# Part of an attention's exponentials on VectorE, a scan in two halves, and zero matmuls sized per group

## The chip, the cores and the metric

One core of a Trainium2 chip. The metric is the device time of one execution in microseconds (us); the median of three runs of the kernel before is 1030.11 us (1026.20 to 1030.48). TensorE does the matrix products and writes to PSUM, ScalarE the exponentials, VectorE most of the elementwise work; SyncE's queue (SP) issues nearly all transfers.

## What is computed

The output mixes two branches of one input `x` (2048 positions, 512 channels) by a gate per position:

```python
g = sigmoid((x * gate_w).sum(-1, keepdims=True))
# a: attention, 32 heads of 16 channels
q, k, v = split(x @ wqkv)
a = (softmax(q @ k.T * 16 ** -0.5) @ v) @ wo
# b: a state-space convolution, 128 complex states for each channel
K[d, l] = sum_n (C * dB)[d, n] * exp(dt * A)[d, n] ** l     # real part
b = causal_conv(x, K) + x * Dskip
return g * a + (1 - g) * b
```

## The kernel before

**Attention.** The 32 heads are worked in 32 blocks of 4 heads by 512 queries. A block has 16 key tiles of 128 keys, and each key tile has four score tiles (one for each head) of 128 keys x 512 queries: 2048 *slots* in all. Three slots make a *group*, 683 groups. `qk` (L662) computes the three score tiles of a group into one of two PSUM banks of 1536 columns, SC0 and SC1, with matmuls that use 32 rows of the array each and run side by side. `ex` (L673, instruction L675) lets ScalarE take the exponential of the whole bank into ET, a ring of 15 tiles (NS). `pv` (L678) multiplies the four tiles of a key tile with the values, 32 columns of the array each, and adds them up in the bank OA over the block; a column of ones among the values gives the sum of the exponentials. At the block's end `norm_a` to `norm_c` (L688 to L697) transpose OA on VectorE, divide, and store to OnT. There is one OA, so the next block's first `pv` waits for `norm_a`.

**State-space branch.** VectorE makes parameters and powers (`params` L756, `base` L854, `table` L892). `kstage` (L946) and `sstage` (L969) form kernels and chunk states with small matmuls into the one shared bank MB, VectorE moves them out (L958, L986, L988), and they go through DRAM. `sload` (L1004) brings the states of a block of 32 channels back, transposed, into SG0 or SG1, which hold a quarter of the channels each. `scan` (L1023) runs 31 steps for each of four quarters on VectorE: G = G * MU + state, complex, in four tensor-tensor instructions of 128x256 fp32 and one cast back to SG (L1040 to L1053). `ystage` (L1090) multiplies the scanned states (SG) and the inputs (X2, loaded by `ublocks` L1139) with the tables, `yread` brings the result back, `combine` and `outs` (L1173, L1195) mix it with the attention's output projection.

**The order of the work** is a list schedule made on the host (`Prog`, `Sched`, L37 to L355). Every instruction has a modelled cost `c` and latency; the program of each engine is then fixed. The main loop (L1325) places, for each group, the exponential, the next score set, and then lets `fill` (L325) pick steps of the other generators that can start by the time ScalarE is modelled to end, by their priority (0 and 1: attention and projections; 2 to 6: the rest). After that it may place zero matmuls (L1342): 128x128 zeros times 512 zero columns, added to OA. They change no value. How many is decided by `lack`: FILL (1400) columns for each group less the weighted columns `a` of the group's own matmuls (512 for a full array, 128 for a score or value matmul), and only while a block's OA is open. All matmuls are issued by L551.

`place` (L462) lays the buffers into SBUF by the groups in which they live; buffers that share bytes add waits.

Of the kernel before, what the change touches and what calls it, by code (L numbers as in the profile page):

```python
# [8 lines left out]
INT32 = mybir.dt.int32  # L9
AF = mybir.ActivationFunctionType  # L10
# [13 lines left out]
FILL = 1400  # L24
NS = 15
SGH = 144
# [3 lines left out]
class Buf:  # L30
# [18 lines left out]
    def int(self, off, dims):  # L49
        return self(off, dims).bitcast(INT32)  # L50

# [4 lines left out]
class Prog:  # L56
# [61 lines left out]
    def ready(self, a):  # L118
        eng, R, W = a[1][0], a[1][2], a[1][3]
        t = 0.0  # L120
        for acc, wr in ((R, False), (W, True)):
            for b, sl, *tag in acc:
# [5 lines left out]
                for d in (st[0], st[1]) if wr else (st[0],):  # L128
                    for s, i in d.items():
                        if s != "PE" or eng != "PE":  # L130
                            t = max(t, self.fin[(s, i)] + (0 if s == eng else .08))
# [29 lines left out]
    def op(self, eng, fn, R=(), W=(), c=.1, lat=.05, a=0):  # L161
# [8 lines left out]
        for s, k in deps.items():  # L170
            at = max(at, self.fin[(s, k)] + (0 if s == eng else .08))
# [63 lines left out]
class Sched:  # L235


    def __init__(self, prog):
        self.p = prog
        self.thr = []  # L240
        self.flag = set()
        self.lock = {}
        self.now = None
        self.n = 0

# [79 lines left out]
    def fill(self, until, pe_until):  # L325
        while True:
            best = None
            for t in self.thr:
# [3 lines left out]
                if t.eng == "PE":  # L332
                    if e + t.cost > pe_until and t.up > 0 or e > pe_until:
                        continue
# [31 lines left out]
def declare(nc, es):  # L366
# [11 lines left out]
    sb("ET", NS * 512)  # L378
    for k in range(4):
        sb(f"OnT{k}", S)  # L380
# [57 lines left out]
    sb("G", 2 * 128, FP32)  # L438
    for n in ("s2", "s3"):
        sb(n, 2 * 128, FP32)  # L440

    sb("X2", 4 * 32 * 64)
# [19 lines left out]
def place(nc, bufs):  # L462
# [20 lines left out]
    for k in range(400):  # L483
# [7 lines left out]
        if best is None or top < best[0]:  # L491
            best = (top, order)
    assert best[0] <= end, (best[0] - end, live(sbs))
# [38 lines left out]
def dv(n, r=1):  # L532
    return .1 + n * 1.045e-3 / r


def record(nc, p, B, ins):
# [10 lines left out]
    MM, QUAD, TRI = .23, .34, .33  # L547
# [85 lines left out]
    def proj_ev(kind, idx, c, bank):  # L633
# [3 lines left out]
           [(o, ky)], c=.65)  # L637

    def vproj_mm(pi, kq, i, q4):
        kt = 4 * kq + i  # L640
        mm(lambda: MB(128 * i, [[1, 128]]), lambda: xT(q4 * S + 128 * kt, [[1, 128]]), lambda: B["Wv"](q4 * D + 128 * pi, [[1, 128]]),
           [xk(kq, q4), (B["Wv"], 0)], [(MB, 0, ('p', "V", pi, kq))], q4 == 0, q4 == 3, c=.08, a=128)

    def vproj_ev(pi, kq):
        op("DVE", lambda v: v.tensor_copy(VE((pi * 16 + 4 * kq) * VW, [[VW, 4], [17, 8], [1, 16]]),
                                          MB(0, [[128, 4], [16, 8], [1, 16]])),
           [(MB, 0, ('p', "V", pi, kq))], [(VE, (pi, 4 * kq + i)) for i in range(4)], c=.68)

    def mk_qm(b):
        qc, pi, w = b // 8, (b % 8) // 2, b % 2  # L650
        op("DVE", lambda v: v.tensor_scalar(Qm(512 * (b % 2), [[1, 512]]), B[f"Q{qc}"](512 * pi, [[1, 512]]),  # L651
                                            msk(w, [[1, 1]]), None, ALU.mult), [(B[f"Q{qc}"], pi), (msk, 0)], [(Qm, b % 2, b)], c=.32)
# [19 lines left out]

    def ex(g):  # L673
        sc, e, n = SC[g % 2], (3 * g) % NS, len(slots(g))
        op("ACT", lambda a: a.activation(ET(512 * e, [[1, 512 * n]]), sc(0, [[1, 512 * n]]), AF.Exp, scale=DH ** -0.5),  # L675
           [(sc, i, g) for i in range(n)], [(ET, s % NS, s) for s in slots(g)], c=.063 + .4267 * n, lat=.1)

    def pv(q):  # L678
        b, kt = divmod(q, 16)
        pi, w = (b % 8) // 2, b % 2  # L680
        for j in range(4):
            hh, e = 2 * j + w, (4 * q + j) % NS
            mm(lambda j=j: OA(0, [[1, 512]], 32 * j, 32), lambda hh=hh: VE((pi * 16 + kt) * VW + 17 * hh, [[1, 32]]),
               lambda e=e: ET(512 * e, [[1, 512]]),
               [(VE, (pi, kt))] + [(ET, (4 * q + i) % NS, 4 * q + i) for i in (range(4) if j == 0 else [j])],
               [(OA, 0, b)], kt == 0, kt == 15, pos=(0, 32 * j), c=QUAD if j == 0 else 0, a=128)

    def norm_a(b):  # L688
        op("DVE", lambda v: v.transpose(OT(0, [[1, 512]]), OA(0, [[1, 512]])), [(OA, 0, b)], [(OT, 0, b)], c=.72)  # L689

    def norm_b(b):
# [3 lines left out]
                                            Rz(16 * w, [[1, 16], [0, 16]]), ALU.mult), [(OT, 0, b), (Rz, w)], [(ON, w)], c=.4)  # L695

    def norm_c(b):  # L697
        qc, pi = b // 8, (b % 8) // 2
        op("DVE", lambda v: v.transpose(OnT[qc](pi * 512, [[1, 512]]), ON(0, [[1, 512]])), [(ON, 0), (ON, 1)],
           [(OnT[qc], pi)], c=.7)  # L700
# [153 lines left out]
    def base(qr, eng):  # L854
# [4 lines left out]
        for l, n in ((0, "VV"), (1, "VL")):  # L859
            yield (eng, .38)  # L860
            op(eng, lambda v, l=l, n=n: v.tensor_copy(FP(l, [[e8, 2], [8, 128]]), B[n](d0, [[D, 2], [1, 128]])), key(n), [(FP, 0)], c=.38)
# [30 lines left out]
    def table():  # L892
# [3 lines left out]
        for pb in range(NBLK // 2):  # L896
# [9 lines left out]
            for i in range(2):  # L906
                yield ("DVE", .4)
                op("DVE", lambda v, i=i, b0=b0, B16=B16: v.tensor_copy(PT(i * PTN, [[CB * T, 2], [T, CB], [1, 16]]),
                                                                     B16(b0 + i * CB * 16, [[2048, 2], [16, CB], [1, 16]])), bk, [W[i]], c=.38)
# [21 lines left out]
    X2 = B["X2"]  # L931
# [37 lines left out]
    def sstage(blk):  # L969
        yield ("AFTER", f"ub{blk // 4}")  # L970
        q0, qr, bl = (blk % 2) * PTN, blk // 4, blk % 4
        for bank in range(4):
# [3 lines left out]
            for pp in range(2):  # L976
                yield ("PE", .29)
                for j in range(4):
                    k, par = 4 * bank + 2 * pp + j // 2, j % 2
                    mm(lambda pp=pp, j=j: MB(256 * pp, [[1, 256]], 32 * j, 32),  # L980
                       lambda k=k, par=par: X2(2048 * qr + 16 * bl + k, [[64, 32]], 64 * par, 64),
                       lambda k=k, par=par: Qt(q0 + 128 * k, [[16 * 128, 2], [1, 128]], 64 * par, 64),
                       [(Qt, (blk % 2, k // 8), blk), (Qt, (blk % 2, 2 + k // 8), blk), (X2, (qr, par))], [(MB, 0, ('S', blk, bank))], pos=(64 * par, 32 * j),
                       c=.29 if j == 0 else 0, a=32)
            yield ("DVE", .8, -1)
            op("DVE", lambda v, bank=bank: v.tensor_copy(Sst(512 * bank, [[256, 2], [1, 128]]), MB(0, [[256, 2], [1, 128]])),  # L986
               [(MB, 0, ('S', blk, bank))], [(Sst, bank, (blk, bank))], c=.37)
            op("DVE", lambda v, bank=bank: v.tensor_scalar(Sst(512 * bank + 128, [[256, 2], [1, 128]]), MB(128, [[256, 2], [1, 128]]),  # L988
                                                           -1.0, None, ALU.mult),
               [(MB, 0, ('S', blk, bank))], [(Sst, (bank, 1), (blk, bank))], c=.37)  # L990
# [13 lines left out]
    def sload(blk):  # L1004
# [3 lines left out]
        if qr < 2:  # L1008
            yield ("AFTER", "K15" if qr else "K3")
        else:  # L1010
            yield ("AFTER", f"yq{qr - 2}")
        sg = SG[qr % 2]
        if bl == 0:
# [3 lines left out]
        dma("SP", lambda e: e.dma_start_transpose(sg(2 * SGH + CB * bl, [[SGH, 64], [1, CB]]),  # L1017
                                                  sd.dram(CB * blk * 8192, [[8192, CB], [1, 8192]])),
            [(sd, (blk, i)) for i in range(4)], [(sg, bl, (qr, 'S'))], c=2.5, lat=3)
# [3 lines left out]
    def scan():  # L1023
# [4 lines left out]
        def quarter(qr):  # L1028
            sg, d0 = SG[qr % 2], 128 * qr
            ks = [(sg, bl, (qr, 'S')) for bl in range(4)]  # L1030
            for bl in range(4):
                yield ("AFTER", f"sg{4 * qr + bl}")
# [367 lines left out]
```

## Time and profile before

| | before |
|---|---|
| median of three runs | 1030.11 us |
| span of the profiled execution (first to last instruction) | 1023.2 us |
| median less span | 6.9 us |
| ScalarE busy | 946.5 us (93%) |
| TensorE busy | 866.9 us (85%) |
| VectorE busy | 611.4 us (60%) |
| mean granted TensorE clock | 0.690 |

The time of the profiled execution itself is not recorded beside its span; the median of the runs is taken as what stands around it. In the profile's rows `PE` is TensorE's matmuls, `PEld` its weight loads, `DVE` VectorE, `ACT` ScalarE, `SP` the queue of most transfers. A stretch's row has its bounds, its length, then for each engine the busy us and (x number of instructions), then the granted clock, the share of the DMA engines and GB/s. A row of a group has line, engine, operation, output <- inputs, shapes and count, then the busy us and the mean ns of one, then the idle time before it and what ended that.

### The profile page before, as it was taken

What the parts mean: (1) busy time and instruction counts of PE and PEld (TensorE: products, weight loads), DVE (VectorE), ACT (ScalarE), POOL (GpSimd) and SP (SyncE); (2) the same over time, 40 slices, a digit from 0 to 9 for tenths busy, and PEclk for the clock granted to TensorE, in tenths of its full rate; (3) what the DMA queues carried; (4) which work ended last, traced back from release to release, by engine and by line L of the source; (5) the groups of instructions that cost most, each with busy time, mean ns of one, the idle gap of its engine ahead of it and who ended that gap; (6) DMA issues with size and microseconds to landing.
All of it is one profiled execution on the core that took longest, in us unless ns stands there. A gap on an engine that the chain in (4) does not pass through costs nothing.

```text
span 1023.2 us, 17025 instructions
## 1 busy us (share of the span) xinstructions
PE 866.9 (85%) x7076; PEld 246.4 (24%) x7076; DVE 611.4 (60%) x1382; ACT 946.5 (93%) x693; POOL 11.9 (1%) x15
## 2 busy tenths in 40 slices
PE   7888788789889888889989899899887787787786
PEld 3332322112112222223323233233211111111111
DVE  4899999987678998878889988702310000000201
ACT  6999999999889999989999999999999899989985
POOL 4000000000000000000000000000000000000000
PEclk9999995555556887655565665755957766767757
DMA  8200005259997788696475725142100000000000
GB/s 180 83 2 1 2 1 83 103 119 202 232 240 176 170 186 208 187 176 165 108 145 145 168 75 148 40 124 48 42 11 11 1 1 1 1 1 1 1 1 21
DMA packets 228940, 92.21 MB, mean 90 GB/s; under 512 B 193408, under 2 KB 216576, under 8 KB 226816
## 3 DMA queue, kind: packets, MB, share of 16 engines
q1 hardware_dynamic: 227136, 90.22, 38.5%
q10 hardware_dynamic: 1728, 0.92, 0.4%
q8 instruction: 55, 0.90, 0.3%
q14 instruction: 21, 0.17, 0.0%
HBM read 27.92 MB, written 35.65 MB: 62 GB/s over the span
## 4 chain that ended last, share of the span: by engine, by line
ACT 51%; PE 41%; DVE 2%; SPq 2%; DMA 2%; issue 2%; ACTq 0%; DVEq 0%
ACT ET L675 51%; PE OA L551 19%; PE SC L551 14%; PE MB L551 9%; SPq L1017 1%; DMA Wq<-in_A_wqkv_dram 1%; DMA Qt<-gm_ptd 0%; SPq L937 0%; DVE Sst L986 0%; DMA Tt<-gm_kpd 0%; DVE Sst L988 0%; DVE OT L689 0%; DVE Kst L958 0%; SPq L994 0%; ACTq L555 0%
## 5 line engine op out<-in xcount | busy, mean ns | idle before, releaser
L675 ACT ACTIVATE ET<-SC 128x1536 bf16<-128x1536 f32 (+1 forms) x683 | 939.4, 1508 | 62.1 <-PE SC L551 55.7
L551 PE MATMUL OA<-ET,VE 128*32 128x512 bf16 x2048 | 268.6, 514 | 117.4 <-ACT ET L675 114.1
L551 PE MATMUL SC<-Qm,KT 32*128 32x512 bf16 x2048 | 353.2, 511 | 11.3 <-ACT ET L675 9.7
L551 PEld LDWEIGHTS SC<-Qm,KT 32*128 32x128 bf16 x2048 | 69.5, 95 | 275.9 <-issue 203.6
L551 PE MATMUL OA<-wm 128*128 128x512 bf16 x276 | 123.5, 573 | 1.2 <-DVE wm L604 1.2
L551 PEld LDWEIGHTS OA<-ET,VE 128*32 128x32 bf16 x2048 | 56.8, 100 | 268.9 <-ACT ET L675 242.0
L651 DVE TENSOR_SCALAR Qm<-Q,msk 128x512 bf16<-128x512 bf16 x31 | 10.6, 342 | 178.7 <-PE SC L551 178.7
L689 DVE STREAM_TRANSPOSE OT<-OA 128x512 f32<-128x512 f32 x32 | 22.9, 714 | 74.2 <-PE OA L551 74.1
L703 DVE TENSOR_TENSOR tt<-B,D 128x1024 bf16<-128x1024 bf16 x96 | 63.2, 683 | 0.3
L1050 DVE TENSOR_TENSOR G<-s,s 128x256 f32<-128x256 f32 x120 | 50.7, 422 | 3.4
L551 PE MATMUL MB<-Qt,X 64*32 64x256 bf16 x512 | 43.3, 392 | 8.8 <-issue 3.2
L1040 DVE TENSOR_TENSOR s<-G,MU 128x256 f32<-128x256 f32 x120 | 50.1, 417 | 0.1
L1046 DVE TENSOR_TENSOR s<-s,SG 128x256 f32<-128x256 f32 x120 | 50.1, 417 | 0.0
L1043 DVE TENSOR_TENSOR s<-G,MU 128x256 f32<-128x256 f32 x120 | 50.0, 417 | 0.0
L551 PE MATMUL MB<-Py,SG 128*32 128x64 bf16 x1024 | 44.1, 259 | 0.0
L1118 DVE CAST Yst<-MB 128x256 bf16<-128x256 f32 x32 | 13.5, 423 | 50.7 <-PE MB L551 50.5
L986 DVE CAST Sst<-MB 128x256 bf16<-128x256 f32 x64 | 27.0, 422 | 24.3 <-PE MB L551 23.8
L551 PEld LDWEIGHTS OA<-wm 128*128 128x128 bf16 x276 | 27.5, 119 | 57.4 <-issue 52.3
L1053 DVE CAST SG<-G 128x256 bf16<-128x256 f32 x120 | 34.9, 291 | 3.0
L551 PE MATMUL MB<-Tt,X 64*32 64x64 bf16 x512 | 35.7, 267 | 0.2 <-DMA Tt<-gm_kpd 0.2
L551 PEld LDWEIGHTS MB<-Py,SG 128*32 128x32 bf16 x1024 | 27.5, 150 | 34.9 <-issue 31.8
L703 DVE TENSOR_TENSOR ft<-FP,L 128x1024 f32<-128x1024 f32 (+1 forms) x32 | 33.8, 1079 | 0.0
(123 smaller groups left out, 470.2 us busy)
## 6 DMA issues: line engine op xcount, KB each, us to landing
gm_ptd<-PT SPq DMA_DIRECT2D x16, 1024.0 KB, 5.1
Py<-gm_ptd SPq DMA_DIRECT2D x32, 512.0 KB, 4.3
gm_sd<-Sst SPq DMA_DIRECT2D x64, 128.0 KB, 2.7
gm_kpd<-Kst SPq DMA_DIRECT2D x16, 256.0 KB, 4.3
Tt<-gm_kpd SPq DMA_DIRECT2D x128, 32.0 KB, 3.5
gm_xrd<-in_A_x_dram SPq DMA_DIRECT2D x1, 2048.0 KB, 12.1
X<-gm_xrd SPq DMA_DIRECT2D x8, 256.0 KB, 4.9
gm_ytd<-Yst SPq DMA_DIRECT2D x32, 64.0 KB, 4.0
```

The source lines that it names most:

```text
L551: op("PE", lambda t: t.matmul(out(), lhsT(), rhs(), start=start, stop=stop, skip_group_check=True, **kw), R, W, c=c, lat=.15, a=a)
L651: op("DVE", lambda v: v.tensor_scalar(Qm(512 * (b % 2), [[1, 512]]), B[f"Q{qc}"](512 * pi, [[1, 512]]), msk(w, [[1, 1]]), None, ALU.mult), ...
L675: op("ACT", lambda a: a.activation(ET(512 * e, [[1, 512 * n]]), sc(0, [[1, 512 * n]]), AF.Exp, scale=DH ** -0.5), [(sc, i, g) for i in ran ...
L689: op("DVE", lambda v: v.transpose(OT(0, [[1, 512]]), OA(0, [[1, 512]])), [(OA, 0, b)], [(OT, 0, b)], c=.72)
L703: op(eng, lambda v: v.tensor_tensor(o(), a(), b_(), f), R, W, c=c)
L986: op("DVE", lambda v, bank=bank: v.tensor_copy(Sst(512 * bank, [[256, 2], [1, 128]]), MB(0, [[256, 2], [1, 128]])), [(MB, 0, ('S', blk, ba ...
L1040: op(e, lambda v: v.tensor_tensor(s2(0, [[128, 2], [1, 128]]), G(0, [[128, 2], [1, 128]]), MU(d0, [[0, 2], [1, 128]]), ALU.mult), key("G", ...
L1043: op(e, lambda v: v.tensor_tensor(s3(0, [[128, 2], [1, 128]]), G(128, [[-128, 2], [1, 128]]), MU(D + d0, [[D, 2], [1, 128]]), ALU.mult), k ...
L1046: op(e, lambda v, so=so: v.tensor_tensor(s2(0, [[128, 2], [1, 128]]), s2(0, [[128, 2], [1, 128]]), sg(so, [[SGH, 2], [1, 128]]), ALU.add), ...
L1050: op(e, lambda v: v.tensor_tensor(G(0, [[1, 256]]), s2(0, [[1, 256]]), s3(0, [[1, 256]]), ALU.add), [(s2, 0), (s3, 0)], [(G, 0)], c=.38)
L1053: op(e, lambda v, so=so: v.tensor_copy(sg(so, [[SGH, 2], [1, 128]]), G(0, [[128, 2], [1, 128]])), key("G"), ks if c < NCH - 2 else [(sg, b ...
L1118: op("DVE", lambda v: v.tensor_copy(Yst(r2 * 256, [[1, 256]]), MB(0, [[1, 256]])), ky, [(Yst, r2, u)], c=.37)
```

## The change

- **Offload.** From group 440 (DV0) on, in two groups of three, and only in key tiles 1 to 13 of a block, the group's third tile is left out of the exponential: 130 tiles, gathered in 34 batches of up to four. For such a tile VectorE writes `XS * score + XB` as 16-bit integers into DZ (`bits`); read as bf16 these bits are 2^e (1 + f). For each batch it then makes m = (1 + f) / 2 with a mask, the product of both, and 2^e (1 + 1/128) with a second mask. The two bf16 terms, product and power, are multiplied with the values one after the other, into the same OA; their sum stands for the exponential. The last value set of a block waits for the block's batches.
- **Scan.** Two halves of 256 channels in place of four quarters of 128: half as many instructions, each twice as wide; SG holds a half. State loads wait for K7 or S15 in place of K3, K15 or the y-stage; X2 is four buffers, loaded one quarter at a time behind the S-stage.
- **Zero matmuls.** The wanted columns follow the modelled time of the group (1600 for 1.335 us); the debt is kept between -256 and 768; MB serves where no OA is open; zeros of 512 or 256 columns; `fill` keeps room for them. In 4 of 14 groups TensorE steps of priority 2 and 5 are held back and at least 1792 columns are wanted.
- Modelled costs and latencies in the schedule are other numbers; the output stage starts at group 480 in place of 400.

The core of the diff:

```diff
-FILL = 1400
+ZCOL = .213 / 512
+FILL = 1600
+OVER = .3
+REST = (14, 4, 1792)
-SGH = 144
+SGH = 272
+NB = 3
+XS = 128 * DH ** -.5 / math.log(2)
+XB = 128 * (127 - math.log2(2 * .7535040986732945))
+DV0 = 440
+DVP = (1, 1, 0)
+DVK = 14
...
+    for g in range(DV0, NG):
+        x = 3 * g + 2
+        if x < NSL and DVP[g % len(DVP)] and 0 < x // 4 % 16 < DVK:
...
     def ex(g):
         sc, e, n = SC[g % 2], (3 * g) % NS, len(slots(g))
+        if 3 * g + 2 in vec:
+            n = 2
...
+    def bits(g):
+        i, k = vec[3 * g + 2]
+        sc, r = SC[g % 2], i % NB
+        op("DVE", lambda v: v.tensor_scalar(DZ.u16(2048 * r + 512 * k, [[1, 512]]), sc(1024, [[1, 512]]), XS, XB, ALU.mult, ALU.add),
+           [(sc, 2, g)], [(DZ, (r, k), (i, k))], c=.61)
...
+    def batch(i):
+        n = 512 * len(order[i]["s"])
+        yield ("DVE", .07 + n / 3840)
+        mask(i, DU, 0x007F, 0x3F00, [(DU, i % NB, ("m", i))])
+        yield ("DVE", dv(n, 2))
+        square(i)
+        yield ("DVE", .07 + n / 3840)
+        mask(i, DZ, 0x7F80, 0x0001, [(DZ, (i % NB, k), (i, k, "t")) for k in range(len(order[i]["s"]))])
+        b = order[i]["b"]
+        yield ("AFTER", f"pv{16 * b}")
...
+        for t in (DU, DZ):
+            yield ("PE", QUAD)
+            for k, s in enumerate(order[i]["s"]):
+                key = (DU, i % NB, i) if t is DU else (DZ, (i % NB, k), (i, k, "t"))
+                pv_mm(s, t, 2048 * (i % NB) + 512 * k, [key], QUAD if k == 0 else 0)
...
-            sg, d0 = SG[qr % 2], 128 * qr
+            sg, d0 = SG[h], 256 * h
...
+            if kt == 15:
+                yield ("AFTER", f"dv{b}")
...
         t = p.tm["ACT"]
-        sch.fill(t, t + .35)
-        lack = min(lack, 1536) + FILL - p.act
-        b = sch.now
-        while lack > 256 and b is not None and p.tm["PE"] < t + .2:
-            mm(lambda: OA(0, [[1, 512]]), lambda: wm(0, [[1, 128]]), lambda: wm(0, [[1, 512]]), [(wm, 0)], [(OA, 0, b)], False, False)
-            lack -= 512
+        want = FILL * (t - t0) / 1.335 + min(max(lack, -256), 768)
+        t0 = t
+        sch.rest = g % REST[0] < REST[1]
+        if sch.rest:
+            want = max(want, REST[2])
+        sch.fill(t, t + OVER, want)
+        lack = want - p.act
+        p.act = 0
+        while lack >= 256 and p.tm["PE"] < t + OVER:
+            b = sch.now
+            if b is not None:
+                bank, W = OA, [(OA, 0, b)]
+            elif sch.lock.get("MB") is None:
+                bank, W = MB, [(MB, 0, "zero")]
+            else:
+                break
+            n = 512 if lack >= 512 else 256
+            mm(lambda bank=bank, n=n: bank(0, [[1, n]]), lambda: wm(0, [[1, 128]]), lambda n=n: wm(0, [[1, n]]), [(wm, 0)], W,
+               bank is MB, bank is MB, c=n * ZCOL, a=n)
+            lack -= n
```

More of the change, by code (lines that the diff above doesn't have):

```diff
@@ L929, in table @@
                 sch.add(kstage(blk), .5)
-    X2 = B["X2"]
+    X2 = [B[f"X2{k}"] for k in range(4)]
     def qload(blk):
@@ L1049, in quarter @@
[L1049 to L1056 removed]
+                yield (e, F5)
```

221 lines of the change are left out of this document (137 added, 84 removed).

## The prediction

> **What bounds the kernel now.** I read the page first: the span, the engines, the clock row, the chain.
>
> ```profile
> span 1023.2 us, 17025 instructions
> PE 866.9 (85%) x7076; PEld 246.4 (24%) x7076; DVE 611.4 (60%) x1382; ACT 946.5 (93%) x693; POOL 11.9 (1%) x15
> PEclk9999995555556887655565665755957766767757
> ACT 51%; PE 41%; DVE 2%; SPq 2%; DMA 2%; issue 2%; ACTq 0%; DVEq 0%
> ```
>
> ScalarE is busy for 93% of the span, yet the chain that ends last gives TensorE 41%: the two alternate, and TensorE's clock is full only at first. Next, the stretches view of the exponential's tile (ET), four stages between changes of clock; behind it the same stages for OA, the bank of the value matmuls and of the zero matmuls.
>
> ```profile
> core 0: us, PE busy (x) PEld busy (x) ACT busy (x), PEclk, DMA share, GB/s
> 14.50:154.90 140.40, 30.83 (x308) 7.93 (x308) 139.47 (x104) 1.00 0.11 27
> 154.90:298.30 143.40, 45.14 (x292) 8.31 (x292) 134.81 (x99) 0.51 0.72 163
> 298.30:650.60 352.30, 99.30 (x716) 20.54 (x716) 331.44 (x239) 0.63 0.70 157
> 650.60:1012.60 362.00, 92.46 (x728) 19.88 (x728) 332.74 (x244) 0.69 0.07 17
> ```
>
> ```profile
> 14.50:154.90 140.40, 30.83 (x308) 7.93 (x308) 3.00 (x5) 1.00 0.11 27
> 154.90:298.30 143.40, 46.17 (x294) 8.44 (x294) 3.56 (x5) 0.51 0.72 163
> 298.30:650.60 352.30, 143.09 (x814) 29.74 (x814) 7.83 (x11) 0.63 0.70 157
> 650.60:1012.60 362.00, 166.12 (x892) 36.66 (x892) 7.89 (x11) 0.69 0.07 17
> ```
>
> Time over exponentials gives each stage's pace: 1.350, 1.448, 1.474, 1.484 us per group of three tiles. At the full clock ScalarE runs end to end at 1.35; the later stages lose 143.4 - 99 x 1.35 = 9.8, 352.3 - 239 x 1.35 = 29.6 and 362.0 - 244 x 1.35 = 32.6 us: **72 us of excess**. The second fence minus the first counts the zero matmuls: 0, 2, 98, 164. So the projections held the clock in stage one, and when they ended nothing replaced them: the fill at L1339 keeps an unlimited debt, and the surplus of the projections postpones zeros for some 150 us.
>
> What one group costs at either clock is in the timeline of TensorE in the last stage, and the chain view says who waits.
>
> ```profile
> 870.22 0.61 PE L551 MATMUL SC<-Qm,KT 32*128 32x512 bf16 x3
> 870.76 1.89 PE L551 MATMUL OA<-wm 128*128 128x512 bf16 x4
> 872.58 0.61 PE L551 MATMUL SC<-Qm,KT 32*128 32x512 bf16 x3
> 873.12 0.41 PE L551 MATMUL OA<-ET,VE 128*32 128x512 bf16 x4
> 873.47 0.39 PE L551 MATMUL SC<-Qm,KT 32*128 32x512 bf16 x3
> ```
>
> ```profile
> ACT ET L675 <- PE SC L551: 55.7, 93, 3.4
> ```
>
> Start to start at half clock: a score set .54 (872.58 to 873.12), a zero 1.82 / 4 = .455; at full clock a set of four value matmuls .35. A burst of four zeros at half clock stands for 1.82 us ahead of the next scores, longer than one exponential: that is the wait of ScalarE, 55.7 us in 93 waits.
>
> **What moves the clock.** Stretches on the grid of the clock changes (3.41 us), all engines, then OA, then ET:
>
> ```profile
> 866.37:869.79 3.42, 1.91 (x22) 0.59 (x21) 0.00 (x0) 2.94 (x3) 0.00 (x0) 1.00 0.00 0
> 869.79:873.20 3.41, 3.41 (x18) 0.73 (x18) 0.00 (x0) 2.54 (x2) 0.00 (x0) 0.50 0.00 0
> 880.03:883.44 3.41, 2.24 (x20) 0.71 (x18) 0.35 (x1) 3.41 (x4) 0.00 (x0) 1.00 0.00 0
> ```
>
> ```profile
> 866.37:869.79 3.42, 1.01 (x13) 0.30 (x12) 0.00 (x0) 1.00 0.00 0
> 869.79:873.20 3.41, 2.46 (x12) 0.52 (x12) 0.00 (x0) 0.50 0.00 0
> 880.03:883.44 3.41, 1.46 (x11) 0.52 (x12) 0.00 (x0) 1.00 0.00 0
> ```
>
> ```profile
> 866.37:869.79 3.42, 0.89 (x12) 0.30 (x12) 2.94 (x3) 1.00 0.00 0
> 869.79:873.20 3.41, 0.58 (x8) 0.09 (x8) 2.54 (x2) 0.50 0.00 0
> 880.03:883.44 3.41, 0.80 (x8) 0.21 (x8) 3.41 (x4) 1.00 0.00 0
> ```
>
> I weigh each matmul by its share of the array: 128 columns for a score or value matmul, 512 for a zero, edges cut off. The first window (tail of one zero) carries about 2,400, and the next runs at half. The second (four zeros) carries about 3,200, and the next is full. The third (three zeros) about 3,400, and the clock stays. So the window's weighted work decides, with an edge between 2,400 and 3,200; I take 2,900 (an estimate), both to hold and to regain the full clock. Own work of 768 a group (six matmuls) gives 768 x 3.41 / 1.35 = 1,940: never enough alone.
>
> **The change part by part.** *Offload.* 130 groups drop their third tile from ScalarE. The lines view by source shows a two-tile exponential (the shortest) beside the usual three:
>
> ```profile
> L675 ACT ACTIVATE ET<-SC x683: 1023/1451/1863, 14.5 to 1012.6; 128x1536 bf16<-128x1536 f32 x171
> ```
>
> 1.451 - 1.023 = .428 us each, x 130 = **-55.6 us**, all in the last stage, provided nothing else sets the pace there.
>
> *New VectorE work.* Rows by shape:
>
> ```profile
> L636 DVE CAST KT<-MB 128x512 bf16<-128x512 f32 x15 | 10.3, 690 | 3.7 <-PE MB L551 3.3
> L741 DVE TENSOR_SCALAR u<-u 128x512 int32<-128x512 int32 x2 | 0.8, 416 | 0.0
> L908 DVE COPY PT<-B 128x1024 bf16<-128x1024 bf16 x16 | 6.3, 419 | 0.8 <-DMA gm_ptd<-PT 0.8
> L703 DVE TENSOR_TENSOR tt<-B,D 128x1024 bf16<-128x1024 bf16 x96 | 63.2, 683 | 0.3
> L1050 DVE TENSOR_TENSOR G<-s,s 128x256 f32<-128x256 f32 x120 | 50.7, 422 | 3.4
> L1053 DVE CAST SG<-G 128x256 bf16<-128x256 f32 x120 | 34.9, 291 | 3.0
> L703 DVE TENSOR_TENSOR u<-u,u 128x512 f32<-128x512 f32 x13 | 8.9, 685 | 0.2
> 650.00:1013.00 363.00, 299.47 (x2065) 76.53 (x2062) 50.64 (x114) 333.74 (x244) 0.00 (x0) 0.69 0.07 17
> ```
>
> The bits instruction reads 512 columns of PSUM: .69 as L636, x 130 = 90 us. The selection makes 34 batches (28 of four tiles, 6 of three). A mask over 2,048 16-bit elements has no row: twice L908 is .84, four times the bitwise L741 is 1.66, four times L636 is 2.76; below it can't be under L908's .42. I take .75, nearest to L908 (same element size, one source); a square is at most 2 x .683, I take 1.25. 34 x (2 x .75 + 1.25) = 94 us. Together 184 us on an engine that is busy for 50.6 of the last 363: 235 of some 290, so it fits, at a cost of 0, hidden by ScalarE's 1.02 to 1.45 per group. If that cover is gone it costs at once: the scores two groups on write the bank that the bits instruction reads, so they now wait for VectorE too, and behind a bits instruction that waits for its scores stand, in order, the batches, the norms and the evictions of MB, for which TensorE waits. The Trainium skill (VectorE: DVE Perf Modes, The perf-mode tier table) gives .693 us for a 2,048-element bf16 tensor_scalar in SBUF; by it the masks cost 47 instead of 51 us and the sum stays. No row here has 16-bit integers.
>
> *Scan on halves.* 120 steps of 4 x .42 + .29 = 1.97 become 60 steps of 4 x .685 plus a cast of .29 to .58 (I take .42): 236 to 190 us, 46 us of VectorE freed. ScalarE's wait list names TensorE alone, so this is worth 0 on the path; it makes room. The 16 state loads wait for more blocks (K7, S15), the 8 loads of X2 go from one burst to behind the S stage of earlier quarters; all stay on SP's queue, none is added, and what they pass there are table and Sst transfers with idle engines beside them after 700 us; the first scan starts later. I take 0, at most +5. The output stage moves from group 400 to 480, with 203 groups left for its 16 tiles: 0.
>
> *Added value matmuls.* 68 extra sets (two terms, 34 batches), 42 of which hit one array position twice: 26 x .35 + 42 x .55 = 32 us at full clock (.55 for two passes, an estimate between .35 and .70), twice that at half. A batch must end before its block's last value set, which waits for it; behind that stand all later scores, in order.
>
> *Sized zeros.* 1,600 columns for each 1.335 modelled us, debt cut to -256..768, MB as second bank, and 4 groups in 14 cleared of prio-2 and prio-5 TensorE steps and raised to 1,792. At full clock a window then carries 1,600 x 3.41 / 1.335 = 4,090, far over 2,900; the time is .35 + .26 + 1.6 x .23 = .98 of 1.35. At half: .54 + .41 + 1.6 x .455 = 1.69 us a group, 3,230 a window: over the edge, so one slow window should cure itself. In the last stage at full clock TensorE needs 243 x .61 = 148, 32 for the terms, and about 230 zeros x .23 = 53: 233 of 271 us.
>
> What is left of the excess: in the first 39.4 us I keep 17, for the waits inside TensorE's order, which the clock doesn't cure:
>
> ```profile
> PE MB L551 <- DVE Sst L988: 5.2, 9, 2.2
> PE MB L551 <- issue: 3.2, 3, 2.5
> PE MB L551 <- DVE Kst L959: 3.0, 6, 0.6
> ```
>
> (11.4 us, and 5.6 for the windows that they cool.) In the last 32.6 us I keep 18: about 1 us at each of 11 block ends, and 7 for two-tile groups, whose 1.02 us leave the next scores less room. So -22 and -15.
>
> **Sum**: 1023.2 - 55.6 - 22 - 15 = 931 us of span. The median of 1030.1 lies 6.9 above this span; 938.
>
> **The rivals.** *A, no excess at all*: 72 + 55.6 go, 1023.2 - 127.6 + 6.9 = 902. For it: stage one does it for 140 us. Against: block ends and late banks. By the Trainium skill (TensorE: Matmul & The Clock Gate, Part 1) one busy window opens the gate and it takes an idle one to close it; then A would hold. The row at 866.37 disagrees: 1.91 us busy of 3.42, in pieces, and the next window is at .50.
>
> *B, the last stage's clock stays at .69*, because batches and block ends keep breaking the windows. At half clock TensorE needs 231 + 62 + 105 = 398 us there, 1.64 a group; mixed by time (.62 half, at 1.64; .38 full, at 1.16) 243 groups take 344 us, 18 less than now: 1023.2 - 22 - 18 + 6.9 = 990.
>
> *C, slower: the zeros are fixed in the program and are paid at half clock.* With S- and y-stage matmuls a half-clock group of the third stage costs about 1.9 us (1.69, and .2 for these, an estimate). Weighted by time the clock is .635 over the last three stages, so half clock holds (1 - .635) / .5 = .73 of it. With that share kept, stage two takes 99 / (.73 / 1.69 + .27 / 1.36) = 157 us, 14 more; stage three 239 / (.73 / 1.9 + .27 / 1.36) = 410, 58 more; the last 344, 18 less: 1023.2 + 54 + 6.9 = **1084**. It decides at a half-clock share of about .5, where the same three quotients add up to the 858 us of now. Against it: 3,230 to 4,090 a window. For it: third-stage groups at half clock carry only 1,600 x 3.41 / 1.9 = 2,870, about the edge.
>
> *D, masks at one element per cycle* (2.76): VectorE needs 235 + 137 = 372 us in the last stage and sets its pace: 938 + 82 = 1020.
>
> **How the numbers follow.** Forecast 938 (918 to 965): .54. A .10, B .14, D .05, C .13, near no change .04. Faster by over .5% (5 us, about what can be told from no change): .54 + .10 + .14 + .05, .83; same .04; slower .13. The range 900 to 1000 leaves out C, D and little else.
>
> **What would show it.** Right: the clock row at 9 from slice 7 on, paces near 1.36 in the middle and 1.17 over groups 440 on, zeros in every stage, the shortest exponential 131 times, ScalarE's idle under 30 us. Wrong: the clock still at .6 to .7 (B, C), VectorE over 9 tenths in the last third with ScalarE's scores waiting on it (D), masks over 1 us, or a stall at each block's end longer than 2 us.

## The result, and the profile after

The changed kernel takes 931.93 us (median of four runs, 924.96 to 932.78) where the kernel before took 1029.59 in the same session: a ratio of 0.905 (95% interval 0.901 to 0.910). The forecast was 938, faster. Rivals B and C, which needed the clock to stay low, are ruled out by the page alone, whose first lines answer to those shown of before:

```profile
span 929.4 us, 18551 instructions
PE 828.3 (89%) x7834; PEld 284.8 (31%) x7834; DVE 742.9 (80%) x1312; ACT 875.4 (94%) x693; POOL 11.7 (1%) x13
PEclk9999999999997878898999999999999999999998
ACT 65%; PE 20%; DVE 6%; DMA 5%; SPq 3%; issue 1%; ACTq 0%; DVEq 0%
```

The clock row stands at 9 but for seven slices (mean 0.966, from 0.690), and TensorE's share of the chain that ended last has fallen from 41% to 20%. The profiled execution itself took 931.17 us, 1.8 more than its span. That settles one term of the prediction: the profile of before was of an execution of about 1023.2 + 1.8 = 1025 us, a quick one, so of the 6.9 us that the sum added, 5.1 were the spread of the runs. Profile against profile the change is 929.4 - 1023.2 = -93.8 us; the prediction's -92 was right to 2 us. Its parts were not, as the stretches view of ET shows, cut where the 1st, 105th, 204th and 443rd exponential start (columns as before):

```profile
11.58:151.57 139.99, 30.56 (x308) 7.93 (x308) 139.15 (x104) 1.00 0.15 36
151.57:288.37 136.80, 29.86 (x300) 7.64 (x296) 134.04 (x101) 0.98 0.66 154
288.37:634.17 345.80, 75.29 (x720) 18.60 (x716) 323.06 (x239) 0.93 0.66 145
634.17:910.05 275.88, 72.43 (x594) 18.07 (x594) 271.94 (x242) 0.99 0.19 47
```

The counts include an exponential that reaches across a bound, so I go by the true 104, 99 and 239 groups. Excess over 1.35 us for a group of three tiles and .922 for one of two, worked out in the same way from the starts of all 683 exponentials, is the currency for the rest of the document:

| us | first start | groups 1-104 | 105-203 | 204-442 | 443-683 | sum of excess | last start to end | span |
|---|---|---|---|---|---|---|---|---|
| before | 14.5 | 0.0 | 12.3 | 30.5 | 34.5 | 77.3 | 10.7 | 1023.2 |
| after | 11.6 | -0.4 | 3.1 | 23.6 | 5.6 | 31.9 | 20.8 | 929.4 |

(The prediction had 72 for the 77: its counts also took in such exponentials, 686 for 683.) So -93.8 is -55.6 from 130 shorter exponentials, -45.4 of excess, -2.9 from an earlier start, and **+10.1 behind the last exponential**, which the prediction had at 0.

The lines view with shapes kept apart has the prices (busy us, mean ns, idle before). Exponentials overlap their neighbours in it, so that their mean of 1,723 ns is not what one costs; 755.0 us for 552 of them is 1.37:

```profile
L725 ACT ACTIVATE ET<-SC 128x1536 bf16<-128x1536 f32 x552 | 755.0, 1723 | 28.0 <-PE SC L585 26.9
L725 ACT ACTIVATE ET<-SC 128x1024 bf16<-128x1024 f32 x131 | 132.7, 1083 | 1.4 <-PE SC L585 0.8
L585 PE MATMUL OA<-wm 128*128 128x512 bf16 x557 | 201.7, 405 | 1.2 <-DVE wm L638 1.2
L585 PE MATMUL OA<-wm 128*128 128x256 bf16 x322 | 91.1, 283 | 0.0
L745 DVE TENSOR_SCALAR DZ<-SC 128x512 uint16<-128x512 f32 x130 | 89.7, 690 | 77.0 <-PE SC L585 75.6
L753 DVE TENSOR_SCALAR DU<-DZ 128x2048 uint16<-128x2048 uint16 x28 | 19.0, 685 | 0.2
L758 DVE TENSOR_TENSOR DU<-DZ,DU 128x2048 bf16<-128x2048 bf16 x28 | 33.9, 1217 | 0.1
L1138 DVE TENSOR_TENSOR s<-s,SG 128x512 f32<-128x512 f32 x60 | 40.9, 682 | 0.0
```

The bits instruction is .690 us (taken: .69), a mask .685 (taken: .75; rival D had 2.76), a product, the prediction's square, 1.217 (taken: 1.25). VectorE and the waits then answer for the cover. First all engines over the last stage, then two rows of the lists of waits:

```profile
634.17:910.05 275.88, 265.22 (x2617) 93.20 (x2617) 199.35 (x316) 271.94 (x242) 0.00 (x0) 0.99 0.19 47
```

```profile
ACT ET L725 <- PE SC L585: 27.8, 33, 3.6
...
PE SC L585 <- ACT ET L725: 50.6, 192, 1.0
```

VectorE (third engine column) is busy for 199 of 276 us and ScalarE for 272; ScalarE's wait for scores fell from 55.7 us in 93 waits to 27.8 in 33. TensorE's score matmuls waited for the exponential before them, and no row of the whole list has them waiting for the bits instruction: that cover held.

### The profile page after: what moved, and what is told of

Same layout as the page of the kernel before. It is cut to its first block, busy times and chain, and to the rows that moved or that the text cites. A ratio compares the mean times of both kernels' runs of the same rounds, so it can differ in the third digit from the quotient of the medians.

```text
span 929.4 us, 18551 instructions
## 1 busy us (share of the span) xinstructions
PE 828.3 (89%) x7834; PEld 284.8 (31%) x7834; DVE 742.9 (80%) x1312; ACT 875.4 (94%) x693; POOL 11.7 (1%) x13
## 4 chain that ended last, share of the span: by engine, by line
ACT 65%; PE 20%; DVE 6%; DMA 5%; SPq 3%; issue 1%; ACTq 0%; DVEq 0%
ACT ET L725 65%; PE OA L585 11%; PE SC L585 6%; PE MB L585 3%; DMA gm_ptd<-PT 3%; DVE tt L797 1%; SPq L1031 1%; DVE PT L797 1%; DMA gm_sd<-Sst 1%; DMA Wq<-in_A_wqkv_dram 1%; SPq L1168 1%; DVE Sst L1080 1%; DMA Qt<-gm_ptd 1%; DVE Sst L1082 0%; DVE OT L783 0%
## 5 line engine op out<-in xcount | busy, mean ns | idle before, releaser
L725 ACT ACTIVATE ET<-SC 128x1536 bf16<-128x1536 f32 (+1 forms) x683 | 868.2, 1600 | 29.4 <-PE SC L585 27.8
L585 PE MATMUL SC<-Qm,KT 32*128 32x512 bf16 x2048 | 272.4, 393 | 57.4 <-ACT ET L725 50.6
L585 PE MATMUL OA<-wm 128*128 128x512 bf16 (+1 forms) x879 | 255.1, 360 | 1.2 <-DVE wm L638 1.2
L585 PE MATMUL OA<-ET,VE 128*32 128x512 bf16 x1918 | 208.5, 399 | 5.4 <-DVE OT L783 5.1
L745 DVE TENSOR_SCALAR DZ<-SC 128x512 uint16<-128x512 f32 x130 | 89.7, 690 | 77.0 <-PE SC L585 75.6
L585 PEld LDWEIGHTS OA<-wm 128*128 128x128 bf16 x879 | 63.4, 98 | 100.6 <-issue 83.4
L797 DVE TENSOR_TENSOR tt<-B,D 128x1024 bf16<-128x1024 bf16 x96 | 63.6, 685 | 0.7
L1141 DVE TENSOR_TENSOR G<-s,s 128x512 f32<-128x512 f32 x60 | 41.3, 689 | 1.6
L1138 DVE TENSOR_TENSOR s<-s,SG 128x512 f32<-128x512 f32 x60 | 41.0, 683 | 0.0
L1135 DVE TENSOR_TENSOR s<-G,MU 128x512 f32<-128x512 f32 x60 | 41.0, 683 | 0.0
L1133 DVE TENSOR_TENSOR s<-G,MU 128x512 f32<-128x512 f32 x60 | 40.9, 682 | 0.0
L758 DVE TENSOR_TENSOR DU<-DZ,DU 128x2048 bf16<-128x2048 bf16 (+1 forms) x34 | 39.4, 1171 | 0.2
L797 DVE TENSOR_TENSOR ft<-FP,L 128x1024 f32<-128x1024 f32 (+1 forms) x32 | 33.7, 1083 | 0.0
L797 DVE TENSOR_TENSOR PT<-tt,tt 128x1024 bf16<-128x1024 bf16 x48 | 32.9, 685 | 0.6
L783 DVE STREAM_TRANSPOSE OT<-OA 128x512 f32<-128x512 f32 x32 | 22.7, 711 | 11.9 <-PE OA L585 11.8
## 6 DMA issues: line engine op xcount, KB each, us to landing
gm_xrd<-in_A_x_dram SPq DMA_DIRECT2D x1, 2048.0 KB, 12.3
```

Of the source, the lines that this page charges most:

```text
L585: op("PE", lambda t: t.matmul(out(), lhsT(), rhs(), start=start, stop=stop, skip_group_check=True, **kw), R, W, c=c, lat=.15, a=a)
L745: op("DVE", lambda v: v.tensor_scalar(DZ.u16(2048 * r + 512 * k, [[1, 512]]), sc(1024, [[1, 512]]), XS, XB, ALU.mult, ALU.add), [(sc, 2, g ...
L758: op("DVE", lambda v: v.tensor_tensor(DU(2048 * r, [[1, n]]), DZ(2048 * r, [[1, n]]), DU(2048 * r, [[1, n]]), ALU.mult), dz(i) + [(DU, r, ...
L797: op(eng, lambda v: v.tensor_tensor(o(), a(), b_(), f), R, W, c=c)
L1133: op(e, lambda v: v.tensor_tensor(s2(0, W), G(0, W), MU(d0, [[0, 2], [1, 256]]), ALU.mult), key("G", "MU"), [(s2, 0)], c=F5)
L1135: op(e, lambda v: v.tensor_tensor(s3(0, W), G(256, [[-256, 2], [1, 256]]), MU(D + d0, [[D, 2], [1, 256]]), ALU.mult), key("G", "MU") + [(M ...
```

## The experiments

All kernels ran beside the kernel before; a ratio is to that. Each expectation says what its theories are; a number of one run alone is marked so.

### 1. The offload taken out

```diff
-DV0 = 440
+DV0 = 10 ** 6
```

> The changed kernel without the offload: no tile goes to VectorE, all exponentials take three tiles; zeros and scan as changed. Theory 1 (the offload is worth its ScalarE time, .428 us x 130 = 55.6, and the zeros do the rest): 932 + 56, less some 8 us of the longer end that VectorE's new work causes, so 975 to 988. Theory 2 (the zeros alone make the gain, and the waits for VectorE eat the offload's): under 950.

972.05 us, ratio 0.942 (0.939 to 0.945), clock .966: theory 2 falls, and the time is just under theory 1's range. Against 931.93 the offload is worth 40.1 us, not 55.6. Two things take the rest: the last stage's excess without it is -0.5 instead of 5.6, and the stretch from the last exponential's start to the end is 11.4 instead of 20.8 (6.1 + 9.4 = 15.5, the whole difference). Where the longer stretch behind the last exponential (the tail) comes from is a step that the lists of y-stage instructions show, the tile view's row for before and for after, then for this run (min/median/max ns, first and last start):

```profile
L1118 DVE CAST Yst<-MB x32: 384/424/425, 463.9 to 708.4; 128x256 bf16<-128x256 f32 x32
L1209 DVE CAST Yst<-MB x32: 407/418/425, 507.2 to 843.1; 128x256 bf16<-128x256 f32 x32
```

```profile
L1209 DVE CAST Yst<-MB x32: 415/424/426, 507.7 to 752.2; 128x256 bf16<-128x256 f32 x32
```

With VectorE loaded and its TensorE steps held back in 4 of 14 groups, the y-stage ends at 843. The 16 output tiles can only start behind it (the first is mixed at 854.1, in before at 717.7); which of the two holds it up is for experiments 6 and 7. After's chain shows what that leaves for the end:

```profile
914.99 0.76 DVE fp L1300
915.75 0.05 issue
915.80 0.83 PE MB L585 x3
916.63 0.03 issue
916.66 0.76 DVE fp L1300
917.42 0.05 issue
917.47 0.83 PE MB L585 x3
```

TensorE and VectorE take turns on the one bank MB at 1.67 us a tile while ScalarE has nothing left. The last block's value matmuls stand behind them in TensorE's order, at 919.9, and its normalisation at 920.7; in before the normalisation began 1.7 us after the last exponential started.

### 2. The changed kernel without its zeros

```diff
-            mm(lambda bank=bank, n=n: bank(0, [[1, n]]), ...)
+            p.tm["PE"] += n * ZCOL
```

> The changed kernel with its order kept but no zero matmul issued in the main loop (they change no value). Theory 1 (the clock follows the weighted columns of a 3.41 us window): own work alone is some 2,000 to 2,300 a window, the clock falls to about .5 after the projections end, TensorE needs 1.0 us of a full group and 1.2 of a two-tile group, so ScalarE loses little in the middle (pace 1.40 to 1.45) and more at the end (pace 1.25 to 1.3 for 1.14): 970 to 995. Theory 2 (the zeros are not what holds the clock; the added value matmuls and the new order are): clock over .9 and 925 to 935.

944.24 us (one run), clock .664. Both theories missed: without zeros the clock falls to about what it was in before, and it costs 12.3 us, not 40 and not nothing (of the profile's 13.0 us, 14.9 are excess, 1.6 a later first exponential, and the tail is 3.4 shorter). Excess of the last stage is 22.2 (5.6 with zeros), of the middle 23.4 (26.7 with zeros).

### 3. The kernel before with the new zeros alone

The new `want`, `lack`, `room` and held-back steps, put into before; X2's loads wait for base2 in place of base1, so that the buffers fit.

> The kernel before with only the new rule for zero matmuls and held-back steps (X2 loaded one step later, for room in SBUF); old scan, no offload, old modelled costs. Theory 1: the clock goes from .69 to over .9, most of the 72 us of excess goes: 965 to 990. Theory 2 (the gain comes from the new modelled costs and order, the zeros cost as much as they give): 1010 to 1040 with the clock under .8.

1012.35 us, ratio 0.982 (0.979 to 0.985), clock .948. Both missed. The excess all but goes, 77.3 to 13.0, yet the span shrinks by only 17.4: the last exponential starts at 947.4, and the end comes 58.5 us later. The tile view again:

```profile
L1126 DVE CAST Yst<-MB x32: 414/424/425, 453.9 to 950.6; 128x256 bf16<-128x256 f32 x32
```

The y-stage runs until 950.6, past the last exponential, because its TensorE steps are among those held back.

### 4. Zeros a quarter as wide

```diff
-mm(lambda bank=bank, n=n: bank(0, [[1, n]]), lambda: wm(0, [[1, 128]]), ...
+mm(lambda bank=bank, n=n: bank(0, [[1, n]], 0, 32), lambda: wm(0, [[1, 32]]), ..., pos=(0, 0), ...
```

> The changed kernel with the same zero matmuls in the same places and of the same length, each 32 output columns wide instead of 128 (they change no value), so that TensorE is as long busy with a quarter of the weighted work. Theory 1 (a window's work weighted by the share of the array decides): some 2,500 a window, the clock falls under .65, the zeros are paid at half clock, 1030 to 1085, slower than before (rival C of the prediction). Theory 2 (being busy decides, as the Trainium skill has it in TensorE: Matmul & The Clock Gate, Part 1): clock over .95 and 925 to 940.

929.96 us (one run), clock .959: theory 1 falls. Page and lines with shapes:

```profile
PEclk9999999899998879899999999999999899989998
...
L585 PE MATMUL OA<-wm 128*32 128x512 bf16 x548 | 197.9, 402 | 0.0
```

The zeros use 32 columns of the array in place of 128, last as long (402 ns against 405), and hold the clock as well. I went back to the windows of 3.41 us in which exponentials run, on the grid of the clock's changes, with the prediction's weight and with the time in which any column streams (columns over the granted clock, overlaps counted once, from every matmul record of the trace). The full clock is set at 2.4 columns a ns, as the Trainium skill has it (TensorE: Matmul & The Clock Gate, Part 1); the traces agree, since at the full clock zeros of 512 columns start .215 us apart at the least (median .216 with narrow zeros, .226 in before), 2.4 columns a ns, and .40 to .43 us apart at half:

| windows | count | weight | us of streaming |
|---|---|---|---|
| before, full, next full | 72 | 2,818-5,282 | 1.44-2.35 |
| before, full, next half | 37 | 1,664-2,764 | 0.89-1.54 |
| narrow, full, next full | 233 | 1,856-5,312 | 1.43-2.78 |
| narrow, full, next half | 10 | 501-2,515 | 0.32-1.44 |
| before, half, next full | 36 | 2,901-3,500 | 2.67-2.98 |
| before, half, next half | 146 | 896-3,021 | 0.87-2.80 |
| narrow, half, next full | 10 | 1,682-2,169 | 2.68-2.92 |
| narrow, half, next half | 10 | 256-2,354 | 0.45-2.83 |

In before alone the weight splits the full windows without a miss, which is why I believed it. With narrow zeros 69 of the 233 that kept the clock lie below 2,764, and each of the ten that regained it lies below before's lowest such window. Streaming time splits both kernels at one place: one full window in each lies on the wrong side of about 1.44 us, and some ten of 182 and three of 20 half windows on the wrong side of about 2.68. Half the clock takes twice the time, so 1.44 us to hold and 2.7 to regain are nearly the same number of columns. Counted in the same way, the other traces blur both edges: the changed kernel kept the clock after windows of 1.29 and 1.41 us, it lost it after one of 1.67 without its zeros (experiment 2), and half windows of 2.2 to 2.6 us were followed by a full one in several runs (2.21 in experiment 6, 2.17 in experiment 9). So these two values are the middle of a band; what makes single windows differ is open. One pair of windows, narrow zeros and before, all engines:

```profile
165.50:168.91 3.41, 3.41 (x22) 0.80 (x18) 3.41 (x8) 2.73 (x2) 0.00 (x0) 0.50 0.00 0
168.91:172.32 3.41, 3.11 (x31) 0.99 (x28) 3.41 (x7) 3.24 (x3) 0.00 (x0) 1.00 0.00 0
```

```profile
163.23:166.64 3.41, 2.59 (x18) 0.54 (x18) 3.38 (x5) 3.41 (x5) 0.00 (x0) 0.50 0.53 84
166.64:170.05 3.41, 2.47 (x17) 0.43 (x13) 3.41 (x6) 3.41 (x3) 0.00 (x0) 0.50 0.97 153
```

The first carries less weight (1,840) than the third (2,105), but TensorE is busy throughout, and only the first is followed by a full window. The same page of the Trainium skill, in the same part, says that a busy window opens the gate: that much the runs bear out, busy time and not width. That it takes an idle window to close it, they don't: windows with up to 1.54 us of streaming close it in before.

### 5. The kernel before without its 267 zeros

```diff
-            mm(lambda: OA(0, [[1, 512]]), lambda: wm(0, [[1, 128]]), ...)
+            p.tm["PE"] += MM
```

> The kernel before, same order, without its 267 zero matmuls of the main loop (they change no value). Theory 1 (new, after the run without zeros in the changed kernel: the excess of before was not half clock in itself but the bursts of four zeros, paid at half clock ahead of the next scores): the last stage's pace falls from 1.49 to 1.40 or less though the clock falls to .6, 990 to 1010. Theory 2 (the prediction's: half clock makes the excess, zeros are its cure): no gain, 1025 to 1045.

996.94 us (one run): theory 1 holds. Taking the zeros away lowers the clock from .690 to .605 and saves 1029.3 - 996.9 = 32 us (28.1 from profile to profile). The last stage of ET, same group bounds, first in before and then here, and ScalarE's wait here:

```profile
654.03:1014.06 360.03, 92.67 (x728) 19.77 (x724) 330.87 (x241) 0.70 0.07 17
649.88:985.90 336.02, 107.28 (x728) 20.38 (x728) 328.30 (x242) 0.56 0.07 18
```

```profile
ACT ET L675 <- PE SC L551: 32.1, 63, 3.7
```

24 of the 28.1 us come from this stage, where its excess falls from 34.5 to 10.5. Most of what I called "excess from the low clock" there was the bursts of zeros themselves, issued at half clock in front of scores. What is left to the low clock is at most the remaining 10.5 us. It is not so in the stage before: there about 100 zeros went and the excess fell from 30.5 to 26.5 only.

### 6. The y-stage ahead of the held-back steps

```diff
-(ystage(), 2)
+(ystage(), 1.5)
```

A priority of 1.5 takes it out of the steps that are held back, and puts it ahead of the other steps of priority 2 as well; experiment 7 shows the first alone. First in the changed kernel:

> The changed kernel with the y-stage at priority 1.5 for 2, so that it is not held back in 4 of 14 groups and goes ahead of the zeros. Theory 1 (the 20.8 us behind the last exponential, 10.7 before, are the state-space branch that ends late: y-stage to 843 us, output tiles to 920): the end falls to 11 to 14 us, 920 to 926. Theory 2 (VectorE, full of offload work, delays the output tiles whatever the y-stage does): 929 to 935.

919.36 us, ratio 0.893 (0.888 to 0.897), clock .975: theory 1 holds, a little better than its range, and theory 2 falls, since VectorE has the same work (743.8 us busy, 742.9 in after). The y-stage ends at 755.9 (tile view below), and the tail is 10.4 us again. Against experiment 1 it is 972.05 - 919.36 = 52.7 us; as experiment 1 has the y-stage in its old place, that is not the offload alone.

```profile
L1209 DVE CAST Yst<-MB x32: 386/424/426, 502.4 to 755.9; 128x256 bf16<-128x256 f32 x32
```

Then in experiment 3 (before with the new zeros):

> The kernel before with the new rule for zeros (1012, of which 58.5 us stand behind the last exponential) and the y-stage at priority 1.5 for 2, so that it is not held back. Theory 1 (in the old order the last two quarters' states wait for the y-stage of the first two, so holding the y-stage back delays the scan to 804 us and the end with it; the zeros alone are worth the rest): the end falls to 11 to 15 us, 962 to 975. Theory 2 (the end is long because VectorE has the longer scan to do): 1000 to 1015.

964.20 us, ratio 0.938 (0.931 to 0.944), clock .976: theory 1 holds, and 47 of the 58.5 us of tail are gone (11.1 left). In the old order the states of quarters 2 and 3 aren't loaded before the y-stage lets go of the buffers of quarters 0 and 1, so a y-stage that is held back holds the scan back too (last cast to SG at 804.0 in experiment 3, 740.1 here, 658.8 in before). The changed kernel's scan on halves doesn't: its scan ends at 603.4 and 601.8 with either priority.

This run is also the closest comparison for the scan and its loads: old scan, new zeros, no offload, 964.20, against 972.05 for experiment 1 with the new scan; the intervals of the ratios overlap. The two differ in the y-stage's priority and the modelled costs too, so they don't give the scan's worth by itself. In its middle stages it has 11.6 us of excess, where experiment 1 has 26.5.

### 7. No held-back groups

```diff
-REST = (14, 4, 1792)
+REST = (14, 0, 1792)
```

(X2's last quarter waits two S-stage steps longer, so that the buffers fit.)

> The changed kernel with no groups cleared and raised to 1792 columns (1600 everywhere; X2's last quarter loaded two steps later, for room in SBUF). Theory 1 (1600 columns hold the clock by themselves, and clearing the groups only delays the y-stage): clock within .02 of .966, end of 12 to 15 us, 920 to 930. Theory 2 (the cleared groups are what brings the clock back in the middle): clock under .9, 940 to 965.

925.43 us, ratio 0.897 (0.893 to 0.901), clock .947: theory 1 holds. 1,600 columns hold the clock by themselves. With the y-stage at its old priority and nothing held back it ends at 740.0, and the tail is back at 10.7 us: so it is the holding back that made the tail, with VectorE loaded (experiment 1 holds back too, without the offload, and its tail is 11.4). The profiled execution (933.68, the longest of the five) has 11.2 us more excess than after, most of it in groups 105-203 (11.9 against 3.1).

### 8. The y-stage first, no zeros

Experiments 2 and 6 together.

> The changed kernel with the y-stage at priority 1.5 (919) without its zero matmuls, order kept. Theory 1 (half clock by itself costs little, since a group's own work is about 1.0 us at half clock; what costs is a burst of zeros paid at half clock): 930 to 940 at a clock of .6 to .7. Theory 2 (the full clock is worth the prediction's 37 us and more): over 950.

936.74 us, ratio 0.910 (0.906 to 0.914), clock .688: theory 1 holds. The zeros are worth 17.4 us in this order, 16.1 of them in the last stage (excess 19.2 against 3.1).

### 9. The scan in 128-wide steps

Experiment 1 with two passes of half width over each half: 120 steps in place of 60, everything else as there.

> To be read against the changed kernel without the offload (972): the same with the scan run 128 channels at a time over the same halves, twice the instructions, about 40 us more of VectorE. Theory 1 (with ScalarE at its pace the state-space branch is the second path, so VectorE's time shows at the end): the time behind the last exponential grows from 11 to over 25, 985 to 1010. Theory 2 (the prediction's: VectorE's time is hidden, worth 0): 968 to 977.

975.67 us, ratio 0.947 (0.942 to 0.952), against 0.942 (0.939 to 0.945): 3.6 us, and the first exponential starts 2.3 us later, which isn't the scan. The prediction's 0 stands. The lines view has the old price, paid twice as often:

```profile
L1144 DVE TENSOR_TENSOR G<-s,s 128x256 f32<-128x256 f32 x120 | 50.8, 423 | 3.4
```

### 10. What stalls the middle

Five groups of after lose 2.2 to 3.8 us each, at 283.9, 308.7, 333.4, 365.4 and 430.2 us. The chain around the third:

```profile
329.29 6.30 DMA gm_ptd<-PT
335.59 0.02 issue
335.61 0.43 DVE PT L1002
336.04 0.33 DVE Sst L1080
336.37 0.34 DVE Sst L1082
336.71 0.14 issue
336.85 0.65 PE MB L585 x7
```

VectorE may copy into PT only when a table's store has landed (6.30 us after its issue), the eviction of MB stands behind that copy, TensorE waits for MB (3.83 us) and the next scores stand behind its matmuls. The second and fourth have such a store in their chain too (8.12 and 6.42 us). The first has some 8 us, most of it VectorE's own table arithmetic (L797), between a store and the eviction, and the last a load of Qt (5.04 us): the five don't have one cause. Two runs tried which resource makes the store late. First, state loads as plain copies in 64-byte pieces:

> The changed kernel with the 16 transposing loads of the chunk states as plain copies of as many bytes (the states land in another order, so the state-space part of the output is not the reference's); order and modelled costs kept. Theory 1 (the five stalls of 2.2 to 3.8 us between 280 and 440 us come from SP's queue: a transposing load holds it for 2.5 to 4.3 us, eight stand in a row, and the stores that free Sst and PT wait behind them): the excess of groups 205 to 310 falls from 25 to under 10, 912 to 920. Theory 2 (the stalls come from VectorE's own order): 928 to 935.

970.67 us, ratio 0.943 (0.938 to 0.948). Both theories missed, since the plain copies were no cheaper transfers: 11.2 us to land where the transposing ones took 5.2, and the second scan waited 19.0 us for one (issues, then VectorE's waits).

```profile
SG<-gm_sd SPq DMA_DIRECT2D x16, 512.0 KB, 11.2
```

```profile
DVE G L1130 <- DMA SG<-gm_sd: 26.4, 2, 19.0
```

So it doesn't tell the queue from the transfer engines. Second, experiment 6 with the schedule told the measured costs:

```diff
-yield ("SP", 2.5) ... c=2.5, lat=3      # state load
+yield ("SP", 3.5) ... c=3.5, lat=3
-[(PT, i, blk)], [(ptd, blk)], c=.5, lat=5
+[(PT, i, blk)], [(ptd, blk)], c=.5, lat=8
```

> The changed kernel with the y-stage at priority 1.5 (919) and two modelled transfers nearer to their rows: a state load 3.5 us of SP's queue for 2.5, a table store 8 us to land for 5. Theory 1 (the stalls of 2 to 5 us between 280 and 430 us come from table stores that land 6.4 to 8.5 us after issue, behind state loads of 3.6, while the order was planned for 5 and 2.5): the excess of groups 205 to 310 falls from 18 to under 10, 905 to 913. Theory 2 (the engines of the transfers are full there whatever the order): 916 to 924.

916.97 us, ratio 0.891 (0.887 to 0.895), against 0.893 (0.888 to 0.897): no difference that can be told, in theory 2's range; its reason isn't shown by that. The third stage's excess is 19.0 where it was 18.9. The four stalls of experiment 6 (2.0 to 4.8 us) are now two, of 5.9 and 11.8 us, and the chain into the longer one has other names in it:

```profile
350.51 1.49 SPq L1031
...
352.18 3.87 SPq L1108
...
356.73 5.65 DMA X<-gm_xrd
362.38 0.04 issue
362.42 0.65 PE MB L585 x6
```

A state load (3.87 us on SP's queue) delays a load of X2, which the S-stage waits for (MB<-Qt,X; the y-stage starts at 507.5 only). So here the wait has moved along SP's queue rather than gone. What would remove it, and whether the transfer engines are the limit, stays open: no run here had fewer transfers at that time.

## Why the prediction was right, and where it wasn't

- **Offload, -55.6.** The size is right (130 x .428; the row of two tiles has 131 of them), and so is the cover: scores never waited for VectorE's read. Of it, 15.5 us were lost again: 6.1 as excess of the last stage, which the prediction had in its 18, and 9.4 in the tail.
- **New VectorE work, 184 us hidden.** Right: 89.7 for the bits, 44.6 for the masks, 39.6 for the products, 174 in all. Rival D fell with the mask's .685. It was not free where TensorE's steps are held back as well: there it moved the y-stage's end from 752 to 843 us (experiment 1).
- **Scan on halves, 0.** Right for the time that VectorE saves (experiment 9). What the prediction didn't see is that the wider scan frees the states from the y-stage: 972 against 1012 us with the y-stage held back (experiments 1 and 3, which differ in the modelled costs too). With the y-stage in front the old scan does as well (964).
- **Sized zeros hold the clock.** Right in effect (.966; rivals B and C fell), for a wrong reason. The failed step is "I weigh each matmul by its share of the array": the gate counts busy time (experiment 4). The two weights give the same answer for full-width zeros, so that the forecast survived by luck. Rival A, no excess at all, fell too: 31.9 us of it are left although the clock was held.
- **The last stage's excess, 32.6 to 18.** Mis-sized: 34.5 to 5.6. The step behind it, one us lost per block end and 7 for short groups, was too dear (the pace over the last stage is 1.14, the sign was 1.17). And the low clock was not what the 34.5 paid for: about 24 of it was zero bursts at half clock (experiment 5). It is with the offload that the full clock pays: without zeros the same stage has 22.2 (experiment 2).
- **The middle's excess, 39.4 to 17.** Mis-sized the other way: 42.8 to 26.7. The sign "paces near 1.36 in the middle" didn't come: 1.38 and 1.45. Nor did the clock make the 16 us that were gained: without zeros, at .664, the middle has 23.4 (experiment 2). Five stalls of 2 to 4 us remain, where before had two (2.9 and 2.5 us). On the old scan, loads and modelled costs the new zeros bring the middle down to 8.6 and 11.6 (experiments 3 and 6, second kernel), so with the zeros in, the new order is about 15 us worse there than the old one, although without them it is 15 better (23.4 against 38.9 in experiment 5). Which part of it does which stays open.
- **The output stage from group 480, "with 203 groups left for its 16 tiles: 0".** Wrong: +10.1. The tiles are released by the y-stage, not by the group number, and the y-stage ended at 843 us in place of 708 (experiments 6 and 7 take the tail away). The prediction counted held-back steps as clock gained and didn't follow what stands behind them.
- **The total** came within 6.1 us by cancellation. Against the sum's -92.6: +5.9 in the middle (-16.1 for -22), +10.1 in the tail, -13.9 in the last stage (-28.9 for -15), -2.9 at the start, -.4 in the first stage, together -1.2, which gives the -93.8; the other 5 us are the quick profiled execution of before.

The best kernels of the study are the first of experiment 6 and the last of experiment 10, 919.36 and 916.97 us, ratios of 0.893 and 0.891 that can't be told apart. The offload on top of experiment 6's second kernel (old scan) was not run, nor were experiments 6 and 7 together, nor the new modelled costs by themselves.

## What to carry to other kernels

A filler that is meant to keep a clock up is itself paid at the low clock, in the order of the program: before counting what the clock would give, take the filler out and see what it costs (here 32 us). When a change holds work back or shortens the path that bounds, follow the second path to its end: the stretch behind the last instruction of the bounding engine shows at once what has become late. A rule fitted to one kernel's trace may rest on quantities that go together there; a run that separates them costs little.

## What the runs showed of the hardware

- Zeros of 32 columns hold TensorE's clock as well as zeros of 128 (.959 and .966). In before and with narrow zeros about 1.44 us of streaming in 3.41 keeps it and about 2.7 at half clock regains it; single windows of other runs lie off by .2 to .5.
- Without zeros, at granted clocks of .605 to .688, these kernels have only 10.5 to 22.2 us of excess in the last stage.
- A mask over 2,048 16-bit integers takes .685 us, a product of two rows of 2,048 bf16 1.217.
- Copies of 512 KB in 64-byte pieces land in 11.2 us, the transposing loads of the same data in 5.2.
